# First block transpose behind the next step's sums, three thresholds taken from GpSimd, and the last batch's exponent step reordered, in a spectral-filter and soft-MoE kernel

## The chip, the core and the metric

The kernel runs on one core of a Trainium2 chip. The core has a matmul engine (TensorE, PE in the profile; its weight loads are listed apart as PEld), VectorE (DVE), ScalarE (ACT), GpSimd (POOL) and SyncE (SP), which here does nothing but issue transfers. The engines run their own instruction streams in order and wait for one another by semaphores. The metric is device time in microseconds (us) of one execution of the whole program; of several executions the median counts.

## The reference

Input `x` is 8 batches of 2496 tokens with 256 features.

```python
X = np.fft.rfft(x, axis=1)                       # along the tokens
Yr = Xr @ w_r - Xi @ w_i + b_r                   # 256 x 256 weights
Yi = Xr @ w_i + Xi @ w_r + b_i
Y  = sign(Y) * max(abs(Y) - 0.01, 0)             # on Yr and Yi apart
y  = np.fft.irfft(Y, n=2496, axis=1)             # 19968 x 256 when stacked
logits = y @ phi                                 # 32 slots, 4 for each of 8 experts
d = softmax over all 19968 tokens of logits
slot_input = d.T @ y
slot_out[e] = max(slot_input[e] @ w1[e], 0) @ w2[e]
c = softmax over the 32 slots of logits
out = c @ slot_out
```

## The kernel before

**Tiling.** The transform over 2496 tokens is split into one of 39 and one of 64 points. A batch b is 11 units of the first (`a_unit`, PE products `pa`, copied from PSUM to the SBUF tile `ast`, stored to DRAM as `adr`), then 5 steps of the second, each for 4 of the 20 frequencies k1 that are kept. Steps are numbered s = 5b + grp, with grp 0 to 4, 40 in all; in the tile names of an order listing `rt_1_0` is the tile of grp 1, half e = 0. Every batch but the first has its first-transform units run while the steps of the batch before run.

**A step.** `f2` makes the products `px` (two halves c of the features) from `ap`, which comes back from `adr`. ACT copies one part of `px` to `xsm` and rounds all of it to `xth`; DVE adds the other part to `xsm` ("the sums") and puts the rounding rest into `xtl`; POOL rounds `xsm` to `xsh` and puts the rest into `xsl`. Each product of 32-bit numbers is made of three products of rounded parts, so a rounded part and its rest always come in pairs (`xh`, `xl` of the input too: ACT writes `xh`, POOL `xl`). `lin_k` makes `pk` (12 matmuls from `xsh` and `xsl`), `lin_y` makes `py` for each half e of the 256 outputs (12 matmuls for e = 0, as many for e = 1) and DVE joins these and the bias into `ut`. Then comes the threshold sign(u) max(|u| - 0.01, 0), in one of two forms: on POOL, a `TENSOR_SCALAR` that clips `ut` to [-0.01, 0.01] and a `TENSOR_TENSOR` that subtracts this from `ut`; or a relu of `ut` - 0.01 on ACT (`ACTIVATE rt`) and then one `SCALAR_TENSOR_TENSOR` on DVE, min(`ut` + 0.01, relu), "the join". The table entry `lth` gives POOL and ACT in turn: in nearly all steps e = 0 goes the POOL way and e = 1 the ACT way. Only the last steps differ.

**After the threshold.** For the first three groups of the first seven batches the tile `rt` (threshold's result) has its 32 x 32 blocks transposed by a DVE `STREAM_TRANSPOSE` into `z`, one for each e; transfers `y<-z` (16 in a batch, issued by SP in `z_move`) complete the transposition. Of groups 3 and 4, PE transposes `rt` itself (`pt`, copied to `T`). `tp_p` makes the logits in the frequency domain (`pq`, scaled into `p_sb`). When a batch's five steps are through, `c_stages` carries them over to the tokens (`pg`, `pL`), finds the largest logit up to there (`pm`, then `mall` and the diagonal `dg`), spreads it over the partitions with a product with ones (`pb`), subtracts it (`ee`), takes the exponent (ACT `ACTIVATE ee`), goes back to frequencies (`pe`, `pd`, result `dd`) and sums the slots with the products `pr` of `dd` and `y` (or `T`). Of batch 7 `last_chain` does this without transfers between. The soft-MoE's experts and the output follow.

**What sets the order.** Each of these functions is a generator that yields a due time in units of its own (4 for a step, 20 for a batch) and then issues some instructions. A heap takes the earliest due time first. Every engine runs its instructions in the order in which they were issued (`_InOrder`, `sp`, `mm`), so a due time only moves instructions against one another in an engine's row; it delays nothing by itself. The due times are in the table `PLAN`. For this change: `zo`, added for the `z` transposes of e = 0 and e = 1 on top of `tlo`; `late['6']['pb']`, the due time of `pb` of batch 6; `T_['tl']`, the due times of the last step's joins. Helpers record the instructions, so nearly all rows of the profile name three lines: L227 (an instruction of DVE, ACT or POOL), L303 (a matmul) and L297 (a transfer of SP); L645 is a PE transpose.

Of the kernel before, what the change touches and what calls it, by code (L numbers as in the profile page):

```python
# [19 lines left out]
R, G = 3, 22  # L20
# [44 lines left out]
def _constants():  # L65
# [77 lines left out]
PLAN = {  # L143
    "ah": 'A',
    "al": 'P',
    "th": 'PA',
    "sh": 'P',
    "sl": 'P',
    "c0": 0.05,
    "pg": [1.35, 2.3],  # L150
    "pL": [6.6, 7.3],
# [14 lines left out]
    "ko": 0.915,  # L166
    "to": 0.4,
    "ws": [-29, -28.9, -28.8, 2],
    "late": {'6': {'cms': [13.1, 13.2, 18, 22.65, 22.66, 22.67], 'pd': [16.681, 16.6], 'pdt': ('pl', 'pl'), 'pr': [17.15, 18.3, 20.179, 19.707, 19.902], 'pL': [6.6, 7.3], 'pm': 8.51, 'pb': 9.45, 'pe': [11.747, 11.6, 12.419], 'pg': [0.875, 1.275], 'fr': {'sinv': 0, 'm2': 0, 'f1': 0, 'suni': 0}, 'pbx': 1.5, 'pet': ('pf', 'pf'), 'so': 0.2}, '5': {}, '4': {}},
    "T_": {'wl': [[-31, 't', 1], [-29.5, 't', 1], [-27.7, 't', 1], [-25.5, 't', 1], [-23.7, 't', 1], [-21.7, 't', 2], [-20.2, 't', 2], [-19.2, 't', 2], [-18.7, 't', 2], [-18.2, 't', 2], [-15.2, 't', 2], [-14.3, 't', 2], [-13.4, 't', 2], [-12.5, 'c', 2], [-11.8, 's', 1], [-11.2, 'a', 1], [-10.6, 'a', 1], [-10, 'a', 1], [-9.5, 'Ww_r', 1], [-8.7, 'Wnws', 1], [-8.6, 'Wwd', 1], [-6, 'Z', 1], [-5.9, 'Z', 1], [0.01, 'k', 1], [0.01, 'u', 1], [0.02, 'x', 2], [0.02, 'x', 2], [0.02, 'x', 2], [1.4, 'R', 2], [1.4, 'R', 2], [1.73, 'Z', 2], [1.74, 'Z', 2]], 'cl': 2.0, 'cp': 46.5, 'ct': 46.6, 'du': [[2.55, 2]], 'd1': [], 'cm': [19.9, 19.91, 19.92, 25, 25.1, 25.2], 'cm7': [0.71, 1.7, 1.95, 2.7, 2.71, 2.8], 'ye': 0.2, 'te': [[5.6, 0.2], [5.5, 0.4]], 'pg': [-15.49, -11.49, -7.99, -3.934, -2.9], 'yt': 0.578, 'wr': -30.6, 'tp': [0, 0.6, 0.85, 0.5], 'tt': [0.4, 0.55, 0.821, 1.25, 0.994], 'z': 1.686, 'th': [0.1, 0.12], 'tl': [0.2, 0.25], 'pgt': ['ps', 'ps', 'ps', 'pf', 'pf'], 'ch': [0.263, 0.5, 0.7, 1.0, 1.514, 2.0], 'te7': 'AAAAAAAAAA', 'op': 2, 'ot': [3, 5, 7], 'gt': [-14.5, -10.5, -7.0, -3.93, -2.89]},  # L170
    "f1": [-1.6, -1.5],
    "kw": [[-28.6, 4], [-28.4, 12]],
    "ap1": 1.85,
# [57 lines left out]
def fourier_soft_moe_kernel(ctx: ExitStack, tc: tile.TileContext, t: dict, out: bass.AP):  # L231
# [135 lines left out]
    ident, sgn, suni, sinv, dsc, dmask = (cols[k] for k in ("ident", "sgn", "suni", "sinv", "dsc", "dmask"))  # L367
    f1, m2 = cols["f1"][:P1], cols["m2"][:Q1]
# [146 lines left out]
    def moved(s):  # L515
        return s < NZ and s % NGRP < PLAN["nz"]
# [45 lines left out]
    def lin_y(s, e):  # L562
        b, grp = steps[s]
        end = s == ns - 1
        t0 = 4 * s + 1 + (PLAN["T_"]["ye"] if end else 1.35) * e
        yield t0
        py = psum("pl", f"py{b}_{grp}_{e}")
        lin(py, e, 0, xts[(s, 0)], 4 * 64 if grp else WH)
        if e == 1 and not end:
            t0 = 4 * s + 3  # L570
            yield t0
        lin(py, e, 1, xts[(s, 1)], 4 * 64 if grp else WH)
        t0 += 0.55 if e == 0 else PLAN["T_"]["yt"] if end else 0.3
        yield t0
        ks = kss[s]
        ut = wtile([128, KG, 2, 64], F32, "ut", f"ut{b}_{grp}_{e}")
        for ri in range(2):
            V.scalar_tensor_tensor(
                out=ut[:, :, ri, :],
                in0=py[:, ri * 256 : ri * 256 + 256].rearrange("p (j q) -> p j q", q=64),  # L580
                scalar=bcol[:, ri, e : e + 1],
                in1=ks[:, e, :].rearrange("p (j q) -> p j q", q=64),
                op0=ALU.add, op1=ALU.add,
            )
        if s >= NZ + 2:
# [541 lines left out]
    T_ = PLAN["T_"]  # L1127
# [223 lines left out]
    so = [wtile([128, D], F32R, "gp", f"so{i}") for i in range(2)]  # L1351
# [99 lines left out]
```

## Time and profile before

| | |
|---|---|
| median of 3 runs | 524.75 us (524.41, 524.75, 528.37) |
| the profiled execution | 523.68 us |
| its span (first to last instruction) | 521.9 us |
| what lies around the span | 1.8 us |
| busy: PE | 491.3 us, 94% of the span |
| busy: DVE, ACT, POOL | 352.5 us (68%), 327.0 us (63%), 316.6 us (61%) |
| transfers | 130.98 MB, 251 GB/s on the mean |

Busy time is the time in which an engine has an instruction at work. On PE matmuls overlap: a matmul with 256 columns is listed with 0.28 us and starts about 0.12 us behind the one before. A POOL `TENSOR_TENSOR` on 128x512 takes about twice as long as a DVE one of the same size (`xl` 1314 ns, `xtl` 680 ns on the mean).

### The profile page before, as it was taken

The numbers are of one execution on the slowest core, as the hardware profiler recorded it, in microseconds if no ns is written. First come the engines' busy times: TensorE is split into PE (matmuls) and PEld (weight loads), VectorE is DVE, ScalarE is ACT, GpSimd is POOL, SyncE is SP. The second block draws the span as 40 slices with busy tenths as digits, with TensorE's granted clock in tenths as the row PEclk, the third lists the DMA queues.
The fourth block names the chain that finished last, engine by engine and source line by source line (L and its number), as shares of the span: only waits on it lengthen the run. The fifth ranks groups of instructions, "written<-read, shape, count | busy, mean of one in ns | idle before, by whom it ended". The sixth has DMA issues, their size and how long they took to land.

```text
span 521.9 us, 11960 instructions
## 1 busy us (share of the span) xinstructions
PE 491.3 (94%) x4348; PEld 418.3 (80%) x4348; DVE 352.5 (68%) x703; ACT 327.0 (63%) x715; POOL 316.6 (61%) x367
## 2 busy tenths in 40 slices
PE   8887999999999999999999999999999979999991
PEld 4486899899789988998899898979888866468881
DVE  3255785688568866886688667966885686447671
ACT  4346467768666866687668766874565446247771
POOL 0048688778886797689868885887357413214210
PEclk9999899999999999999999999999999999999997
DMA  8998464579847895798589847974899989739998
GB/s 286 325 302 322 156 232 140 163 227 263 271 134 237 257 271 151 220 269 279 135 255 246 280 120 228 265 246 136 230 231 321 238 246 392 293 125 389 405 405 348
DMA packets 90318, 130.98 MB, mean 251 GB/s; under 512 B 40188, under 2 KB 61692, under 8 KB 90260
## 3 DMA queue, kind: packets, MB, share of 16 engines
q1 hardware_dynamic: 89316, 128.10, 76.9%
q10 hardware_dynamic: 944, 2.13, 1.2%
q8 instruction: 34, 0.56, 0.4%
q14 instruction: 24, 0.20, 0.1%
HBM read 69.19 MB, written 50.00 MB: 228 GB/s over the span
## 4 chain that ended last, share of the span: by engine, by line
PE 58%; DMA 15%; POOL 10%; ACT 5%; DVE 5%; issue 3%; SPq 3%; POOLq 0%; ACTq 0%; DVEq 0%
PE py L303 12%; PE pq L303 9%; PE px L303 8%; PE pa L303 8%; PE pk L303 5%; DMA w<-in_moe_w 3%; DMA gd<-g_sb 3%; PE pr L303 3%; POOL xl L227 3%; SPq L297 3%; POOL rt L227 2%; DMA gp<-gd 2%; PE pt L645 2%; POOL xsl L227 2%; PE pc L645 2%
## 5 line engine op out<-in xcount | busy, mean ns | idle before, releaser
L227 POOL TENSOR_TENSOR xl<-xr,xh 117x512 fp32r<-117x512 f32 x73 | 95.9, 1314 | 17.8 <-ACT xh L227 10.0
L303 PEld LDWEIGHTS px<-smov,ap 128*128 128x128 f32 x640 | 80.1, 192 | 10.9 <-ACT ast L227 6.2
L303 PE MATMUL px<-smov,ap 128*128 128x128 f32 x640 | 84.6, 276 | 3.6 <-ACT ast L227 3.6
L227 DVE SCALAR_TENSOR_TENSOR ut<-py,pk,k 128x256 f32<-128x256 f32 x160 | 69.7, 476 | 19.2 <-PE py L303 17.1
L227 POOL TENSOR_TENSOR xsl<-xsm,xsh 128x256 fp32r<-128x256 f32 x77 | 74.0, 961 | 6.3
L227 POOL CAST xsh<-xsm 128x256 fp32r<-128x256 f32 x78 | 34.8, 446 | 66.4 <-DVE xsm L227 53.5
L227 ACT COPY ast<-pa 128x512 f32<-128x512 f32 x82 | 48.4, 591 | 38.9 <-PE pa L303 37.7
L227 DVE STREAM_TRANSPOSE z<-rt 128x512 f32<-128x512 f32 x42 | 29.7, 706 | 38.6 <-POOL rt L227 24.1
L227 DVE TENSOR_TENSOR xtl<-px,xth 128x512 fp32r<-128x512 f32 x80 | 54.3, 680 | 0.1
L227 DVE TENSOR_TENSOR xsm<-px,xsm 128x256 f32<-128x256 f32 x80 | 33.3, 416 | 30.9 <-ACT xth L227 27.4
L303 PE MATMUL py<-xth,nwsh 128*128 128x256 f32 (+1 forms) x160 | 53.1, 332 | 0.4 <-ACT k L227 0.4
L227 ACT CAST xth<-px 128x512 fp32r<-128x512 f32 x80 | 47.3, 592 | 5.1 <-PE py L303 5.0
L227 POOL TENSOR_TENSOR rt<-ut,rt 128x512 f32<-128x512 f32 x39 | 50.1, 1286 | 0.2
L227 ACT COPY xsm<-px 128x256 f32<-128x256 f32 x80 | 30.0, 375 | 28.6 <-PE px L303 20.7
L303 PE MATMUL pk<-xsh,w_rh 128*128 128x256 f32 (+1 forms) x160 | 47.7, 298 | 0.2 <-POOL xsh L227 0.2
L227 ACT CAST xh<-xr 117x512 fp32r<-117x512 f32 x72 | 45.3, 631 | 2.9 <-DMA xr<-in_x 2.9
L303 PE MATMUL py<-xth,wdh 128*128 128x256 f32 (+1 forms) x160 | 45.2, 283 | 0.0
L303 PE MATMUL pk<-xsl,w_rh 128*128 128x256 f32 (+1 forms) x160 | 44.9, 281 | 0.3 <-POOL xsl L227 0.3
L303 PE MATMUL py<-xtl,wdh 128*128 128x256 f32 (+1 forms) x160 | 45.0, 281 | 0.0
L303 PE MATMUL py<-xtl,nwsh 128*128 128x256 f32 (+1 forms) x160 | 45.0, 281 | 0.0
L303 PE MATMUL py<-xth,wdl 128*128 128x256 f32 (+1 forms) x160 | 44.9, 281 | 0.0
L303 PE MATMUL py<-xth,nwsl 128*128 128x256 f32 (+1 forms) x160 | 44.8, 280 | 0.0
(223 smaller groups left out, 1307.0 us busy)
## 6 DMA issues: line engine op xcount, KB each, us to landing
ap<-adr SPq DMA_DIRECT2D x76, 256.0 KB
out<-ost SPq DMA_DIRECT2D x37, 512.0 KB
xr<-in_x SPq DMA_DIRECT2D x35, 512.0 KB
adr<-ast SPq DMA_DIRECT2D x20, 768.0 KB
y<-z SPq DMA_DIRECT2D x112, 96.0 KB
w<-in_moe_w SPq DMA_DIRECT2D x21, 512.0 KB
adr<-ast SPq DMA_DIRECT2D x7, 512.0 KB
w<-in_moe_w SPq DMA_DIRECT2D x14, 256.0 KB
```

Of the source, the lines that this page charges most:

```text
L227: return lambda *a, **k: self.tc.keep_in_program_order(f(*a, **k))
L297: sp_last.append(tc.keep_in_program_order(nc.sync.dma_start(**kw)))
L303: tc.keep_in_program_order(nc.tensor.matmul(**kw))
L645: tc.keep_in_program_order(nc.tensor.transpose(out=out, in_=in_, identity=identity))
```

## The change

Three entries of the table are edited, one is added, and two lines of `lin_y` use them:

- `zo` gets a third value: the first transpose of each batch (grp 0, e = 0) is due 1.5 units later, behind the sums of the step after the next.
- `hA`: 3 is new. In the steps 0, 1 and 2 (all of batch 0) the half e = 0 takes its threshold by ACT and DVE too, in place of POOL.
- `late['6']['pb']`: `pb` of batch 6 is due 0.91 units later.
- `T_['tl'][0]` goes from 0.2 to 0.24: the join of e = 0 in the very last step is due a little later. (The `T_` line is one long row of the table and is left out below.)

```diff
-    "late": {'6': {'cms': [13.1, 13.2, 18, 22.65, 22.66, 22.67], 'pd': [16.681, 16.6], 'pdt': ('pl', 'pl'), 'pr': [17.15, 18.3, 20.179, 19.707, 19.902], 'pL': [6.6, 7.3], 'pm': 8.51, 'pb': 9.45, 'pe': [11.747, 11.6, 12.419], 'pg': [0.875, 1.275], 'fr': {'sinv': 0, 'm2': 0, 'f1': 0, 'suni': 0}, 'pbx': 1.5, 'pet': ('pf', 'pf'), 'so': 0.2}, '5': {}, '4': {}},
+    "late": {'6': {'cms': [13.1, 13.2, 18, 22.65, 22.66, 22.67], 'pd': [16.681, 16.6], 'pdt': ('pl', 'pl'), 'pr': [17.15, 18.3, 20.179, 19.707, 19.902], 'pL': [6.6, 7.3], 'pm': 8.51, 'pb': 10.36, 'pe': [11.747, 11.6, 12.419], 'pg': [0.875, 1.275], 'fr': {'sinv': 0, 'm2': 0, 'f1': 0, 'suni': 0}, 'pbx': 1.5, 'pet': ('pf', 'pf'), 'so': 0.2}, '5': {}, '4': {}},
...
-    "zo": [0.7, 1.0],
+    "zo": [2.2, 0.7, 1.0],
     "nz": 3,
+    "hA": 3,
...
         yield t0 + (PLAN["T_"]["th"][e] if end else PLAN["tho"])
-        relu = L_("th", s, e) is A
+        relu = s < PLAN["hA"] or L_("th", s, e) is A
         if relu:
             A.activation(out=rt, in_=ut, func=AF.Relu, bias=nlam)
...
         if moved(s):
-            yield t0 + PLAN["tlo"] + PLAN["zo"][e]
+            yield t0 + PLAN["tlo"] + PLAN["zo"][0 if grp == e == 0 else e + 1]
```

One line more in the table moves the helpers' lines by one: L227 becomes L228, L303 becomes L304.

DVE in batch 0, from the second `ut` of step 0 on, before:

```order
L227 SCALAR_TENSOR_TENSOR ut_0_1_393<-py_0_1_364,pk_110,k_0_323 128x4x64 x2
L227 STREAM_TRANSPOSE z_404<-rt_0_0_352 128x4x128
L227 TENSOR_TENSOR xsm_2_0_430<-px_2_0_406,xsm_2_0_430 128x256
L227 TENSOR_TENSOR xtl_2_0_429<-px_2_0_406,xth_2_0_428 128x512
L227 SCALAR_TENSOR_TENSOR rt_0_1_396<-ut_0_1_393,rt_0_1_396 128x512
L227 SCALAR_TENSOR_TENSOR ut_1_0_463<-py_1_0_438,pk_110,k_1_436 128x4x64 x2
L227 STREAM_TRANSPOSE z_404<-rt_0_1_396 128x4x128
L227 TENSOR_TENSOR xsm_2_1_502<-px_2_1_468,xsm_2_1_502 128x256
L227 TENSOR_TENSOR xtl_2_1_501<-px_2_1_468,xth_2_1_500 128x512
L227 SCALAR_TENSOR_TENSOR ut_1_1_534<-py_1_1_478,pk_110,k_1_436 128x4x64 x2
L227 TENSOR_TENSOR p_sb_490<-pq_0_491,pk_110 128x128
L227 STREAM_TRANSPOSE z_404<-rt_1_0_466 128x4x128
```

And the same stretch of DVE after:

```order
L228 SCALAR_TENSOR_TENSOR ut_0_1_392<-py_0_1_364,pk_110,k_0_323 128x4x64 x2
L228 SCALAR_TENSOR_TENSOR rt_0_0_352<-ut_0_0_349,rt_0_0_352 128x512
L228 TENSOR_TENSOR xsm_2_0_428<-px_2_0_404,xsm_2_0_428 128x256
L228 TENSOR_TENSOR xtl_2_0_427<-px_2_0_404,xth_2_0_426 128x512
L228 SCALAR_TENSOR_TENSOR rt_0_1_395<-ut_0_1_392,rt_0_1_395 128x512
L228 STREAM_TRANSPOSE z_461<-rt_0_0_352 128x4x128
L228 SCALAR_TENSOR_TENSOR ut_1_0_463<-py_1_0_436,pk_110,k_1_434 128x4x64 x2
L228 STREAM_TRANSPOSE z_461<-rt_0_1_395 128x4x128
L228 TENSOR_TENSOR xsm_2_1_502<-px_2_1_468,xsm_2_1_502 128x256
L228 TENSOR_TENSOR xtl_2_1_501<-px_2_1_468,xth_2_1_500 128x512
L228 SCALAR_TENSOR_TENSOR ut_1_1_533<-py_1_1_478,pk_110,k_1_434 128x4x64 x2
L228 SCALAR_TENSOR_TENSOR rt_1_0_466<-ut_1_0_463,rt_1_0_466 128x512
```

The first transpose (of `rt_0_0`) has moved behind the sums of step 2 and the join `rt_0_1`, and joins `rt_0_0` and `rt_1_0` are new on DVE. `rt_2_0` gets one as well. On POOL the two instructions of each of these three thresholds are gone, and ACT has three `ACTIVATE rt` more.

DVE in batch 2, where its first transpose stands, before:

```order
L227 TENSOR_TENSOR p_sb_1180<-pq_4_1805,pk_110 128x128
L227 STREAM_TRANSPOSE z_1883<-rt_0_0_1784 128x4x128
L227 TENSOR_TENSOR xsm_2_0_1913<-px_2_0_1885,xsm_2_0_1913 128x256
L227 TENSOR_TENSOR xtl_2_0_1912<-px_2_0_1885,xth_2_0_1911 128x512
L227 SCALAR_TENSOR_TENSOR rt_0_1_1861<-ut_0_1_1858,rt_0_1_1861 128x512
L227 SCALAR_TENSOR_TENSOR ut_1_0_1951<-py_1_0_1923,pk_110,k_1_1921 128x4x64 x2
L227 STREAM_TRANSPOSE z_1883<-rt_0_1_1861 128x4x128
```

And after:

```order
L228 TENSOR_TENSOR p_sb_1180<-pq_4_1805,pk_110 128x128
L228 TENSOR_TENSOR xsm_2_0_1911<-px_2_0_1883,xsm_2_0_1911 128x256
L228 TENSOR_TENSOR xtl_2_0_1910<-px_2_0_1883,xth_2_0_1909 128x512
L228 SCALAR_TENSOR_TENSOR rt_0_1_1861<-ut_0_1_1858,rt_0_1_1861 128x512
L228 STREAM_TRANSPOSE z_1949<-rt_0_0_1784 128x4x128
L228 SCALAR_TENSOR_TENSOR ut_1_0_1951<-py_1_0_1921,pk_110,k_1_1919 128x4x64 x2
L228 STREAM_TRANSPOSE z_1949<-rt_0_1_1861 128x4x128
```

Here nothing is added: the transpose changes places with the sums (`xsm`, `xtl`) and the join `rt_0_1`. The batches 1 to 6 all read like this one; POOL's order there is the same as before.

PE at the end of the steps, where `pb` of batch 6 stands, before (from the end of the products `py` of grp 3 on):

```order
L303 MATMUL py_3_1_6291<-xth_3_1_6171,wdl 128x256
L303 MATMUL py_3_1_6291<-xtl_3_1_6172,wdh 128x256
L303 MATMUL pb_6354<-dg_6332,ones 117x32
L645 MATMUL pq_2_6303<-pk_110,lg_2_6345 128x128
L303 MATMUL pk_4_6365<-xsh_4_0_6231,w_rh 128x256
L303 MATMUL pk_4_6365<-xsh_4_0_6231,w_rl 128x256
```

And after, from the last `pk` on:

```order
L304 MATMUL pk_4_6360<-xsh_4_1_6322,w_rh 128x256
L304 MATMUL pk_4_6360<-xsh_4_1_6322,w_rl 128x256
L304 MATMUL pk_4_6360<-xsl_4_1_6323,w_rh 128x256
L304 MATMUL pb_6373<-dg_6332,ones 117x32
L304 MATMUL py_4_0_6385<-xth_4_0_6228,nwsh 128x256
L304 MATMUL py_4_0_6385<-xth_4_0_6228,nwsl 128x256
```

`pb` has moved from ahead of the transposition in `pq` and the 12 `pk` to behind these.

ACT in the same stretch (thresholds of the last steps, exponents `ee` and `fo` of batch 6, the copies `eT` behind the products `pe`), before:

```order
L227 ACTIVATE rt_2_0_6133<-ut_3_1_6349,nlam 128x512
L227 COPY k_4_6383<-pk_4_6365 128x512
L227 ACTIVATE ee_6358<-ee_6358 117x704
L227 ACTIVATE fo<-fo 128x1
L227 ACTIVATE rt_2_0_6133<-ut_4_0_6422,nlam 128x512
L227 COPY eT_6426<-pe_0_6427 128x20x12 x2
L227 COPY eT_6426<-pe_1_6428 128x2x20x3
```

And after:

```order
L228 ACTIVATE rt_2_0_6133<-ut_3_1_6349,nlam 128x512
L228 COPY k_4_6383<-pk_4_6360 128x512
L228 ACTIVATE rt_2_0_6133<-ut_4_0_6420,nlam 128x512
L228 ACTIVATE ee_6375<-ee_6375 117x704
L228 ACTIVATE fo<-fo 128x1
L228 COPY eT_6430<-pe_0_6431 128x20x12 x2
L228 COPY eT_6430<-pe_1_6432 128x2x20x3
```

The relu of the last step's first half now stands ahead of the exponents. On DVE, `p_sb` has moved ahead of `ee` and `fo`, and the last `ut` ahead of the join of the half before it. SP's order is unchanged.

## Rows read from the trace of the kernel before

**Rows 1.** Stretches: us, PE, PEld, DVE, ACT, POOL busy (count), PEclk, DMA share, GB/s

```profile
52.50:57.00 4.50, 4.50 (x19) 4.07 (x20) 2.33 (x5) 1.10 (x2) 2.99 (x4) 0.62 0.44 179
115.00:167.00 52.00, 50.95 (x471) 45.60 (x470) 37.79 (x76) 36.87 (x80) 40.80 (x45) 1.00 0.76 226
374.00:433.00 59.00, 54.29 (x598) 46.87 (x597) 42.40 (x88) 31.62 (x79) 29.36 (x39) 1.00 0.91 262
```

**Rows 2.** Waits of PE between 40 and 63 us: total, times, longest

```profile
PE pa L303 <- DVE ast L227: 1.8, 1, 1.8
PE pa L303 <- ACT k L227: 1.5, 1, 1.5
```

**Rows 3.** Waits of PE between 130 and 370 us

```profile
PE px L303 <- ACT ast L227: 3.4, 5, 0.7
PE pa L303 <- POOL xl L227: 0.8, 3, 0.3
```

**Rows 4.** Chain that ended last, batch 0: start, us, what

```profile
46.90 0.58 POOL rt L227
47.48 1.26 POOL xl L227
...
49.16 0.72 POOL xsl L227
49.88 1.24 POOL rt L227
...
51.78 0.66 DVE ast L227
...
52.48 0.97 PE pa L303 x3
```

**Rows 5.** Timeline, batch 2: start, us, engine, operation, [idle before, releaser]

```profile
137.04 0.59 ACT L227 CAST xth<-px 128x512 fp32r<-128x512 f32 x1
...
138.51 0.72 POOL L227 TENSOR_TENSOR dd<-dd,pk 128x320 f32<-128x320 f32 x1
...
139.19 1.29 POOL L227 TENSOR_TENSOR xl<-xr,xh 117x512 fp32r<-117x512 f32 x1
...
140.31 0.71 DVE L227 STREAM_TRANSPOSE z<-rt 128x512 f32<-128x512 f32 x1 [3.88 <-DMA y<-z]
...
141.86 0.67 DVE L227 SCALAR_TENSOR_TENSOR rt<-ut,rt 128x512 f32<-128x512 f32 x1
141.88 1.24 POOL L227 TENSOR_TENSOR xsl<-xsm,xsh 128x256 fp32r<-128x256 f32 x1
```

**Rows 6.** Tile `xsl` on POOL: ns shortest/median/longest, first and last start

```profile
L227 POOL TENSOR_TENSOR xsl<-xsm,xsh x77: 727/746/1257, 36.1 to 414.1; 128x256 fp32r<-128x256 f32 x77
```

**Rows 7.** Timeline, batch 6, the same place

```profile
347.13 0.91 DVE L227 SCALAR_TENSOR_TENSOR rt<-ut,rt 128x512 f32<-128x512 f32 x1
347.45 1.17 POOL L227 TENSOR_TENSOR dd<-dd,pk 128x320 f32<-128x320 f32 x1
```

**Rows 8.** Timeline, last steps and behind them

```profile
420.91 0.39 PE L303 MATMUL pb<-dg,ones 128*117 128x32 f32 x2 [1.04 <-DVE dg L227]
...
421.16 0.87 DVE L227 SCALAR_TENSOR_TENSOR ut<-py,pk,k 128x256 f32<-128x256 f32 x2
...
422.70 0.28 PE L303 MATMUL py<-xth,nwsh 128*128 128x256 f32 x1
...
423.44 0.80 ACT L227 ACTIVATE ee<-ee 117x704 f32<-117x704 f32 x1
...
424.42 0.88 DVE L227 SCALAR_TENSOR_TENSOR ut<-py,pk,k 128x256 f32<-128x256 f32 x2 [0.73 <-ACT fo L227]
...
425.33 0.72 ACT L227 ACTIVATE rt<-ut,nlam 128x512 f32<-128x512 f32 x1 [1.00 <-DVE ut L227]
...
425.63 0.62 PE L303 MATMUL pe<-pk,ee 117*32 117x120 f32 x16
...
433.02 1.29 PE L303 MATMUL pr<-y,dd 128*32 128x256 f32 x20 [0.20 <-DMA w<-in_moe_w]
```

More of the change, by code (lines that the diff above doesn't have):

```diff
@@ L168 @@
     "ws": [-29, -28.9, -28.8, 2],
-    "late": {'6': {'cms': [13.1, 13.2, 18, 22.65, 22.66, 22.67], 'pd': [16.681, 16.6], 'pdt': ('pl', 'pl'), 'pr': [17.15, 18.3, 20.179, 19.707, 19.902], 'pL': [6.6, 7.3], 'pm': 8.51, 'pb': 9.45, 'pe': [11.747, 11.6, 12.419], 'pg': [0.875, 1.275], 'fr': {'sinv': 0, 'm2': 0, 'f1': 0, 'suni': 0}, 'pbx': 1.5, 'pet': ('pf', 'pf'), 'so': 0.2}, '5': {}, '4': {}},
-    "T_": {'wl': [[-31, 't', 1], [-29.5, 't', 1], [-27.7, 't', 1], [-25.5, 't', 1], [-23.7, 't', 1], [-21.7, 't', 2], [-20.2, 't', 2], [-19.2, 't', 2], [-18.7, 't', 2], [-18.2, 't', 2], [-15.2, 't', 2], [-14.3, 't', 2], [-13.4, 't', 2], [-12.5, 'c', 2], [-11.8, 's', 1], [-11.2, 'a', 1], [-10.6, 'a', 1], [-10, 'a', 1], [-9.5, 'Ww_r', 1], [-8.7, 'Wnws', 1], [-8.6, 'Wwd', 1], [-6, 'Z', 1], [-5.9, 'Z', 1], [0.01, 'k', 1], [0.01, 'u', 1], [0.02, 'x', 2], [0.02, 'x', 2], [0.02, 'x', 2], [1.4, 'R', 2], [1.4, 'R', 2], [1.73, 'Z', 2], [1.74, 'Z', 2]], 'cl': 2.0, 'cp': 46.5, 'ct': 46.6, 'du': [[2.55, 2]], 'd1': [], 'cm': [19.9, 19.91, 19.92, 25, 25.1, 25.2], 'cm7': [0.71, 1.7, 1.95, 2.7, 2.71, 2.8], 'ye': 0.2, 'te': [[5.6, 0.2], [5.5, 0.4]], 'pg': [-15.49, -11.49, -7.99, -3.934, -2.9], 'yt': 0.578, 'wr': -30.6, 'tp': [0, 0.6, 0.85, 0.5], 'tt': [0.4, 0.55, 0.821, 1.25, 0.994], 'z': 1.686, 'th': [0.1, 0.12], 'tl': [0.2, 0.25], 'pgt': ['ps', 'ps', 'ps', 'pf', 'pf'], 'ch': [0.263, 0.5, 0.7, 1.0, 1.514, 2.0], 'te7': 'AAAAAAAAAA', 'op': 2, 'ot': [3, 5, 7], 'gt': [-14.5, -10.5, -7.0, -3.93, -2.89]},
@@ new lines @@
+    "late": {'6': {'cms': [13.1, 13.2, 18, 22.65, 22.66, 22.67], 'pd': [16.681, 16.6], 'pdt': ('pl', 'pl'), 'pr': [17.15, 18.3, 20.179, 19.707, 19.902], 'pL': [6.6, 7.3], 'pm': 8.51, 'pb': 10.36, 'pe': [11.747, 11.6, 12.419], 'pg': [0.875, 1.275], 'fr': {'sinv': 0, 'm2': 0, 'f1': 0, 'suni': 0}, 'pbx': 1.5, 'pet': ('pf', 'pf'), 'so': 0.2}, '5': {}, '4': {}},
+    "T_": {'wl': [[-31, 't', 1], [-29.5, 't', 1], [-27.7, 't', 1], [-25.5, 't', 1], [-23.7, 't', 1], [-21.7, 't', 2], [-20.2, 't', 2], [-19.2, 't', 2], [-18.7, 't', 2], [-18.2, 't', 2], [-15.2, 't', 2], [-14.3, 't', 2], [-13.4, 't', 2], [-12.5, 'c', 2], [-11.8, 's', 1], [-11.2, 'a', 1], [-10.6, 'a', 1], [-10, 'a', 1], [-9.5, 'Ww_r', 1], [-8.7, 'Wnws', 1], [-8.6, 'Wwd', 1], [-6, 'Z', 1], [-5.9, 'Z', 1], [0.01, 'k', 1], [0.01, 'u', 1], [0.02, 'x', 2], [0.02, 'x', 2], [0.02, 'x', 2], [1.4, 'R', 2], [1.4, 'R', 2], [1.73, 'Z', 2], [1.74, 'Z', 2]], 'cl': 2.0, 'cp': 46.5, 'ct': 46.6, 'du': [[2.55, 2]], 'd1': [], 'cm': [19.9, 19.91, 19.92, 25, 25.1, 25.2], 'cm7': [0.71, 1.7, 1.95, 2.7, 2.71, 2.8], 'ye': 0.2, 'te': [[5.6, 0.2], [5.5, 0.4]], 'pg': [-15.49, -11.49, -7.99, -3.934, -2.9], 'yt': 0.578, 'wr': -30.6, 'tp': [0, 0.6, 0.85, 0.5], 'tt': [0.4, 0.55, 0.821, 1.25, 0.994], 'z': 1.686, 'th': [0.1, 0.12], 'tl': [0.24, 0.25], 'pgt': ['ps', 'ps', 'ps', 'pf', 'pf'], 'ch': [0.263, 0.5, 0.7, 1.0, 1.514, 2.0], 'te7': 'AAAAAAAAAA', 'op': 2, 'ot': [3, 5, 7], 'gt': [-14.5, -10.5, -7.0, -3.93, -2.89]},
```

## Prediction

> **What bounds the kernel now.** I read first the busy shares by stretch. PE is busy 50.95 of 52 us in a stretch of one batch (115 to 167 us) [rows 1], at a granted clock of 1.00, which is its 2.4 GHz level; DVE, ACT and POOL stand at 71 to 78% of it. So a change of DVE's or POOL's order counts only where PE waits, or comes to wait. The second view is PE's waits. In 130 to 370 us, nearly five batches, they are small: 3.4 us for `px` behind `ast`, 0.8 us for `pa` behind POOL's `xl` [rows 3]. The first is the turnaround of a copy and lies on ACT, which the change doesn't touch there. The second tells that POOL's row reaches PE at one place in some batches, with nothing to spare. In batch 0, 40 to 63 us, PE waits 1.8 us in one piece for `pa` behind DVE's copy `ast`, and 1.5 us for `k` on ACT [rows 2]. The third view, the chain that ended last, says what the 1.8 us are: POOL `xl` from 47.48, `xsl` from 49.16, the subtraction `rt` from 49.88 for 1.24; to 51.12; then DVE `z`, whose `ast` follows at 51.78, and PE `pa` at 52.48 [rows 4]. DVE stood idle in front of `z`, with `ast` queued behind it. Right behind, from 52.50 to 57.00, the granted clock is 0.62 on the mean, PE at its lower level (1.2 GHz) for much of it [rows 1].
>
> **Thresholds of batch 0 (`hA`).** Three thresholds leave POOL (six instructions) and become an `ACTIVATE` (0.72 us, [rows 8]) and a join on DVE (0.67, [rows 5]) each. What counts is `rt_1_0`, the tile that this `z` waited for. By the new order DVE has this join right behind `ut` and `p_sb` of the step. POOL's clip, 0.58 us at 46.90 [rows 4], no longer stands ahead of `xl`, so `xl` that ended at 48.74 (47.48 + 1.26) ends at about 48.15. The join reads two tiles in SBUF, as do POOL's `TENSOR_TENSOR`s, and rows 5 and 7 show that these don't run side by side; so I let it run behind `xl`, 48.15 to 48.8, then `z` (0.71) to 49.5 and `ast` (0.66) to 50.15. POOL's `xsl` stays about where it was, ending at 49.88, as the 0.6 us gained go to the join. PE is at `pa` only when the products `pk` behind `xsl` are through, at about 50.7 (52.48 less the wait of 1.8). `ast` is there some 0.5 us before. So **-1.8 us** of wait.
>
> With it the clock: 4.5 us at 0.62 lose (1 - 0.62) x 4.5 = 1.7 us [rows 1]. The dip stands just behind this wait, and ahead of it is also the 1.5 us for `k`, which stays. I take it that without the 1.8 us the dip goes: **-1.7 us**; the other bound is 0 (it comes anyway, behind the wait for `k`). The three `ACTIVATE`s lie on an engine that waits for PE's `pk` there (`k` follows `pk`) and cost nothing; if one came in front of `k`, 0.72. Batch 0: **-3.5 us**, between -1.1 and -3.5.
>
> **First transposes behind the sums (`zo`).** In batches 2 to 5 the transpose `z` waits for its tile (`y<-z` transfers of the batch before must have left it), 3.88 us of idle DVE in batch 2, ending at 140.31 [rows 5]; behind it stand the sums, `xsm`, `xtl`, and the join. These are what the move sets free. But who waits for them? POOL takes `xsh` only behind a second `dd` that follows `xl` (139.19 + 1.29), so the sums some 3 us sooner are of no use to it, and `px`, `pk` and `py` of the next step are far from late. So I cost the gain on PE at nothing; the cover is POOL's own row, which is busy without a gap from `dd` to `xl` to `dd` here. If that cover were gone, `pa <- xl` is what could improve, 0.8 us in all [rows 3].
>
> What comes with it: the sums now start when ACT's `xth` is there, at 137.63 (137.04 + 0.59), take 1.0 together (`xtl` 0.68 on the mean, `xsm` has half its elements) and so the join falls to about 138.65. Before, it ran at 141.86, against `xsl`, which took 1.24 us instead of the usual 0.75 [rows 5, 6]. Now it meets POOL's `dd` (138.51 for 0.72) and stands ahead of `xl` (139.19), for which PE waits [rows 3, 5]. The same meeting can be seen in batch 6 as it is: the join at 347.13 has 0.91 us, as it starts while `xl` still runs, and `dd` at 347.45 then 1.17 instead of 0.72 [rows 7]. So the join, if it comes while `dd` runs, waits for its end and then holds up `xl` by what it lasts. From the rows the price of one such meeting is 1.24 - 0.746 = 0.50 us [rows 5, 6], and PE has no slack ahead of `xl`. By where the rows stand I count this in batches 2, 3, 4 and 6; in batch 5 `xl` has already started, and in batch 1 the transpose waits for POOL's `rt` and hardly at all. **+2.0 us** (4 x 0.50). The bounds: 0 (the join slips into a gap, or `xl` is first and `pa` starts on time), and five whole joins, 5 x 0.67 = 3.4 us.
>
> The Trainium skill ("SBUF — State Buffer", section "Who interferes with whom") says that a DVE instruction with two SBUF inputs contends with a GpSimd instruction that reads SBUF, and that whoever comes first has the shared ports for the whole instruction while the other is fully blocked. The rows agree that one waits, but `xsl` lost 0.50 us and not the 0.67 of the join. By the rule to the letter the four meetings would cost 4 x 0.67 = 2.7 us, by the row 2.0; it speaks against this part of the change either way.
>
> **The tail (`pb`, `tl`).** `pb` made PE wait 1.04 us at 420.91 [rows 8]. Behind the 12 `pk` its `dg` is long there. But the gain is not that 1.04: `py` of the last step, which came at 422.70, needs the PSUM bank that `ut` leaves at 422.03 (421.16 + 0.87), so it comes at about 422.07: -0.63. Then on ACT: the relu of the last step's first half now stands ahead of the exponents. Its 12 `py` from 422.07 on, 0.12 apart, end at 423.7, so `ut` (0.88) at about 424.6; the relu takes 0.72 to 425.3, `ee` 0.80 to 426.1, and `pe`, which started at 425.63, waits for `ee` and comes at 426.1: **+0.48 us**. This shift runs on to `pr` at 433.02. That one waited 0.20 us for a transfer of weights [rows 8], so 0.2 are absorbed: **+0.3 us**, bounds -0.6 (the relu ends as early as `py` gains) and +0.5.
>
> **Sum.** -3.5 + 2.0 + 0.3 = -1.2 us against the profiled 523.68, of which 521.9 are span: 522.5. The median of the runs is 1.07 us above the profiled execution, so the forecast is **523.5 us**. A measurement of this kernel tells 1%, 5.2 us, from no change (below 519.5 or above 530.0): by this, no change.
>
> **Rivals.** All on the median, 524.75.
>
> - *The meetings don't bite.* The join finds POOL between two instructions, or `xl` is first. For it: in batch 5 that is what I expect, and a join that came 0.6 us later would do no harm to `xl`; against: POOL has no gaps there [rows 5]. -3.5 + 0.3: 521.5 us. Chance 22%.
> - *The move also clears PE.* With the sums early, POOL's row comes loose and the waits for `xl` vanish too (-0.8, [rows 3]); the tail gains its whole wait, -1.04. -3.5 - 0.8 - 1.04 = -5.3: 519.4 us. Against: POOL waits for nothing but itself in rows 5. Chance 8%.
> - *Transfers take it all.* From 374 to 433 the transfers stand at 0.91 of the 16 engines, and `pr` waited for a landing [rows 1, 8]. If the weights land no sooner, what PE gains or loses before is made up there, and only the tail's rest shows: 525.0 us. Against: 0.20 us is a short wait, and the loads' start hangs on buffers that come free earlier too. Chance 12%.
> - *Slower: the join in front of `xl`.* The mechanism of the +2.0, at its full price in all five batches from 2 to 6 (3.35), with the tail at +0.5 and the clock still falling in batch 0 (-1.8 there): +2.05, 526.8 us. It decides from the point where the meetings cost more than batch 0 gives, seven at 0.50, or the five with the clock not won back. Chance 10%.
> - *`hA` doesn't do its work.* The wait of `pa` stays, since the join `rt_1_0` is held by POOL up to behind `xsl` (49.88) and `z` and `ast` end only at 51.9, or ACT's relu is late. Then the 1.8 shrinks to 0.5, the clock falls: -0.5 + 2.0 + 0.3: 526.5 us. Chance 5%.
>
> **Numbers.** The forecast has 43%: with its own bounds some 522 to 525. The range of 519.8 to 526.9 holds all cases but the second rival and the outer end of the slower ones. Faster by over 1%: half of the second rival, and what of the first ends as low, 0.07. Slower by over 1% needs meetings at more than twice their price: 0.03. Within 1%: 0.90.
>
> **What would show it.** In the profile after: no wait of `pa` behind `ast` around 50.5 us, and PEclk near 1.00 in 52 to 57; if the wait is gone and the clock still falls, the 1.7 were wrong. In batches 2 to 6: DVE's idle time ahead of the first `z` gone, the join next to `dd` with one of them stretched, and PE's waits for `xl` grown from 0.8 to nearly 3 us; if they stay at 0.8, the meetings don't bite. In the tail: no wait at `pb`, a wait of about 1 us at `pe` for `ee`, `pr` behind 433.0 by as much as the rest doesn't shift it. The prediction is wrong as a whole if PE's waits in 130 to 370 us fall instead of rising, or if the time behind 433 us, which the change doesn't touch, differs.

## The result: 1.2% faster, and the profile after

The changed kernel takes 519.38 us at the median of 6 runs (517.36 to 520.09); the kernel before took 524.58 us at the median of 6 (523.77 to 528.37). The ratio of the mean times is 0.9882, 95% interval 0.9847 to 0.9917. Here and below, a ratio leaves out executions that took over 1.5% longer than the fastest of their kernel, and a median does not. The profiled execution took 519.74 us, its span is 517.9 us, against 523.68 and 521.9 before. The forecast of 523.5 us was too high, and the time lies below its range.

PE's order is the same in both kernels but for the one `pb`, so each matmul of the trace after has its partner in the trace of before. The difference of their starts, read along the program, tells where time came from or went. At these places (named by their time before) it is, in us:

| before, us | 49.94 `pk` | 56.93 `px` | 115.9 `px` | 348.9 `px` | 415 | 433.0 `pr` | last matmul |
|---|---|---|---|---|---|---|---|
| changed kernel | -2.32 | -5.92 | -5.60 | -7.69 | -4.53 | -3.91 | -3.86 |

**Batch 0.** PE's waits between 40 and 63 us, and the stretch behind the place of the old wait (columns as in rows 1), in the kernel after:

```profile
PE pk L304 <- POOL xsl L228: 0.3, 1, 0.3
```

```profile
48.30:52.80 4.50, 4.50 (x37) 4.11 (x39) 3.32 (x7) 2.17 (x5) 3.36 (x4) 1.00 0.81 320
```

Both waits of [rows 2] are gone, and PEclk is 1.00 where it was 0.62 [rows 1]. The chain that ended last, in the kernel after, goes through PE itself now, where it went through POOL and DVE [rows 4]:

```profile
46.84 0.74 POOL xsl L228
...
47.62 0.74 PE pk L304 x4
48.35 0.70 PE pa L304 x3
49.05 1.42 PE py L304 x12
```

From 49.94 to 56.93 this is -3.60 us. The -2.32 ahead of it are another thing: ACT's `xh` waited for a transfer there, 2.91 us in the execution before and 1.62 us in this one, and the wait for `k` hangs on it. In the traces of the twelve other kernels below this place lies between -1.04 and +1.42 us, with and without each of the edits, so the -2.32 can't be put down to the change.

**The steady stretch.** PE's waits in the kernel after from 125 to 365 us (the work of 130 to 370 before):

```profile
PE pa L304 <- POOL xl L228: 2.1, 3, 0.8
PE pL L304 <- ACT chpL L228: 1.1, 2, 1.0
PE pd L304 <- POOL clpd L228: 0.3, 1, 0.3
```

The waits for `xl` rose from 0.8 to 2.1 us, as forecast. But the five of `px` behind `ast`, 3.4 us [rows 3], are gone. The timeline of batch 2 after shows both (compare rows 5):

```profile
133.01 0.68 DVE L228 TENSOR_TENSOR xtl<-px,xth 128x512 fp32r<-128x512 f32 x1
133.46 0.72 POOL L228 TENSOR_TENSOR dd<-dd,pk 128x320 f32<-128x320 f32 x1
...
133.61 1.12 DVE L228 SCALAR_TENSOR_TENSOR rt<-ut,rt 128x512 f32<-128x512 f32 x1
...
134.14 1.72 POOL L228 TENSOR_TENSOR xl<-xr,xh 117x512 fp32r<-117x512 f32 x1
...
135.92 0.50 PE L304 MATMUL pa<-xl,f1h 117*128 117x512 f32 x1 [0.77 <-POOL xl L228]
...
136.48 1.06 PE L304 MATMUL px<-smov,ap 128*128 128x128 f32 x8
...
136.68 0.58 ACT L228 COPY ast<-pa 128x512 f32<-128x512 f32 x1 [1.55 <-PE pa L304]
```

The meeting is there as foretold: the join comes at `dd`, lasts 1.12 us, and `xl` 1.72 instead of 1.29. But then `px` starts at 136.48, before the copy `ast` has even begun (136.68). So `px` can't have needed that copy in this kernel. In the kernel before, the same matmuls stood like this:

```profile
140.53 0.50 PE L303 MATMUL pa<-xl,f1h 117*128 117x512 f32 x1 [0.33 <-POOL xl L227]
...
141.26 0.67 DVE L227 TENSOR_TENSOR xtl<-px,xth 128x512 fp32r<-128x512 f32 x1
141.31 0.59 ACT L227 COPY ast<-pa 128x512 f32<-128x512 f32 x1 [1.14 <-PE pa L303]
...
141.95 1.16 PE L303 MATMUL px<-smov,ap 128*128 128x128 f32 x8 [0.68 <-ACT ast L227]
```

From `pa` to `px` it was 1.42 us and is 0.56 now: 0.86 us less, and 0.82 to 0.94 less in each of the other four batches (3 to 6). Note that `xtl` (141.93) and `ast` (141.90) both ended just ahead of `px`.

**The tail.** In the kernel after, timeline:

```profile
414.31 0.32 PE L768 MATMUL pm<-pk,mx 117*128 117x117 f32 x1 [0.51 <-ACT gT L228]
...
417.66 0.36 PE L304 MATMUL py<-xth,nwsh 128*128 128x256 f32 x1 [0.64 <-DVE ut L228]
...
420.36 0.72 ACT L228 ACTIVATE rt<-ut,nlam 128x512 f32<-128x512 f32 x1 [1.62 <-DVE ut L228]
420.99 0.77 ACT L228 ACTIVATE ee<-ee 117x704 f32<-117x704 f32 x1
...
421.82 1.34 PE L304 MATMUL pe<-pk,ee 117*32 117x120 f32 x48 [1.08 <-ACT ee L228]
```

No wait at `pb`; instead `py` waits for `ut` and `pe` for `ee`, behind the relu [rows 8]. Between 348.9 and 415 the changed kernel gives back 3.2 us in this execution: `pd` of batch 5 waits three times, 1.7 us together (one of 0.7 us stood there before too), the first as its input `eb` comes late from DRAM, and then PEclk is 0.50 for 3.40 us, which is 1.7 us lost:

```profile
383.57 0.46 ACT L228 CAST chpd<-eb 128x320 fp32r<-128x320 f32 x1 [3.06 <-DMA eb<-ed]
```

```profile
386.70:390.10 3.40, 3.40 (x18) 3.39 (x17) 1.14 (x3) 1.59 (x4) 3.32 (x4) 0.50 1.06 260
```

### The profile page after: what moved, and what is told of

Read it like the earlier page. It is cut to its first block, busy times and chain, and to the rows that moved or that the text cites. A ratio compares the mean times of both kernels' runs of the same rounds, so it can differ in the third digit from the quotient of the medians.

```text
span 517.9 us, 11977 instructions
## 1 busy us (share of the span) xinstructions
PE 490.0 (95%) x4348; PEld 418.9 (81%) x4348; DVE 360.1 (70%) x706; ACT 328.4 (63%) x718; POOL 311.5 (60%) x361
## 4 chain that ended last, share of the span: by engine, by line
PE 61%; DMA 15%; POOL 8%; DVE 5%; ACT 4%; issue 2%; SPq 2%; ACTq 0%; POOLq 0%; DVEq 0%
PE py L304 13%; PE pq L304 9%; PE px L304 9%; PE pa L304 8%; PE pk L304 6%; PE pr L304 3%; DMA eb<-ed 3%; POOL xl L228 2%; DMA w<-in_moe_w 2%; SPq L298 2%; DMA ed<-ea 2%; PE pt L646 2%; PE pc L646 2%; DMA gd<-g_sb 2%; POOL rt L228 2%
## 5 line engine op out<-in xcount | busy, mean ns | idle before, releaser
L228 POOL TENSOR_TENSOR xl<-xr,xh 117x512 fp32r<-117x512 f32 x73 | 96.8, 1327 | 15.3 <-ACT xh L228 8.1
L304 PEld LDWEIGHTS px<-smov,ap 128*128 128x128 f32 x640 | 81.2, 193 | 5.8 <-ACT ast L228 0.7
L304 PE MATMUL px<-smov,ap 128*128 128x128 f32 x640 | 85.0, 277 | 0.3 <-ACT ast L228 0.3
L228 DVE SCALAR_TENSOR_TENSOR ut<-py,pk,k 128x256 f32<-128x256 f32 x160 | 69.5, 475 | 20.1 <-PE py L304 17.6
L228 POOL CAST xsh<-xsm 128x256 fp32r<-128x256 f32 x78 | 36.0, 462 | 67.7 <-DVE xsm L228 53.0
L228 POOL TENSOR_TENSOR xsl<-xsm,xsh 128x256 fp32r<-128x256 f32 x77 | 72.1, 936 | 6.3
L228 ACT COPY ast<-pa 128x512 f32<-128x512 f32 x82 | 48.3, 590 | 36.1 <-PE pa L304 34.9
L228 DVE TENSOR_TENSOR xsm<-px,xsm 128x256 f32<-128x256 f32 x80 | 33.4, 417 | 42.2 <-ACT xth L228 35.8
L228 DVE TENSOR_TENSOR xtl<-px,xth 128x512 fp32r<-128x512 f32 x80 | 54.2, 679 | 0.1
L304 PE MATMUL py<-xth,nwsh 128*128 128x256 f32 (+1 forms) x160 | 53.0, 331 | 1.0 <-DVE ut L228 0.6
L228 ACT CAST xth<-px 128x512 fp32r<-128x512 f32 x80 | 47.3, 592 | 5.1 <-PE py L304 5.1
L304 PE MATMUL pk<-xsh,w_rh 128*128 128x256 f32 (+1 forms) x160 | 48.1, 300 | 0.0
L228 ACT CAST xh<-xr 117x512 fp32r<-117x512 f32 x72 | 45.4, 632 | 1.6 <-DMA xr<-in_x 1.6
L228 POOL TENSOR_TENSOR rt<-ut,rt 128x512 f32<-128x512 f32 x36 | 46.3, 1287 | 0.1
L304 PE MATMUL pk<-xsl,w_rh 128*128 128x256 f32 (+1 forms) x160 | 45.3, 283 | 0.4 <-POOL xsl L228 0.3
L304 PE MATMUL py<-xth,wdh 128*128 128x256 f32 (+1 forms) x160 | 44.9, 281 | 0.0
L304 PE MATMUL pk<-xsh,w_rl 128*128 128x256 f32 (+1 forms) x160 | 44.9, 281 | 0.0
L304 PE MATMUL py<-xtl,nwsh 128*128 128x256 f32 (+1 forms) x160 | 44.8, 280 | 0.0
L304 PE MATMUL py<-xtl,wdh 128*128 128x256 f32 (+1 forms) x160 | 44.7, 280 | 0.0
L304 PE MATMUL py<-xth,nwsl 128*128 128x256 f32 (+1 forms) x160 | 44.7, 279 | 0.0
L304 PE MATMUL py<-xth,wdl 128*128 128x256 f32 (+1 forms) x160 | 44.6, 279 | 0.0
L228 ACT COPY xsm<-px 128x256 f32<-128x256 f32 x80 | 30.0, 375 | 23.0 <-PE px L304 15.3
```

What stands on the lines that cost most here:

```text
L228: return lambda *a, **k: self.tc.keep_in_program_order(f(*a, **k))
L304: tc.keep_in_program_order(nc.tensor.matmul(**kw))
```

## Why px no longer waits: another PSUM bank

The order of the instructions doesn't show it, but the built programs do (the lists `SECOND` below are made from them): in batches 2 to 6 the second half's `px` of grp 2 lies in another PSUM bank. PSUM is the memory that PE writes its products to. Tiles of the tag `pf` share two banks, and the pool picks one for each tile when it is issued. Before, that `px` got the bank of `pa` and waited for its copy `ast`. After, it gets the bank of the first half's `px`, and has to wait for what reads this, the sums last. With the transpose moved, the pool picks differently, and from there on the two banks are swapped for many later tiles; a swap of both by itself only renames them. My theory then: **the steady gain is this bank together with the early sums**; the meetings at `xl` take part of it. Rivals: batch 0 gives all of the gain; or the early sums help without the bank, or the bank without them.

## Experiments

Ratios are to the kernel before, timed on the same chip in turn.

**Each edit alone.** `z_alone` has the `zo` edit only:

```diff
-    "zo": [0.7, 1.0],
+    "zo": [2.2, 0.7, 1.0],
-            yield t0 + PLAN["tlo"] + PLAN["zo"][e]
+            yield t0 + PLAN["tlo"] + PLAN["zo"][0 if grp == e == 0 else e + 1]
```

> Only the first transpose of each batch is moved (zo); thresholds and tail as before. Theory (early sums give PE's px its PSUM bank sooner): the five waits of px behind the copy ast (3.4 us in 130 to 370 us, 0.85 us each from start to start in the trace of after) go, three to four waits for POOL xl grow by 0.45 us each, so about -2.5 us: 522.1 us. Rival (the steady stretch gains nothing by this edit, all of the gain comes from batch 0): between 0 and +2 us, as the prediction had it: 524.6 to 526.6 us, with the waits of px still there.

Measured: 0.9956 (0.9925 to 0.9988), -2.3 us. PE's waits, 125 to 365 us, have no `px` behind `ast`, and more of `xl`:

```profile
PE pa L303 <- POOL xl L227: 2.3, 3, 0.8
PE px L303 <- DMA ap<-adr: 1.1, 1, 1.1
```

From 115.9 to 348.9 its trace gains 2.19 us, as the changed kernel's does (2.09). The edit that I had put at +2.0 us is a gain.

`h_alone` has the `hA` edit only:

```diff
+    "hA": 3,
-        relu = L_("th", s, e) is A
+        relu = s < PLAN["hA"] or L_("th", s, e) is A
```

> Only the three thresholds of batch 0 are moved to ScalarE and VectorE (hA). Theory: PE's wait of 1.8 us for pa behind ast in batch 0 goes and the dip of the granted clock behind it with it: -3.5 us, 521.1 us; the five waits of px in 130 to 370 us stay at 3.4 us. If the 1.5 us for k is shortened by this edit too (it is gone in the trace of after), -4.5 to -5 us: 519.9 us. Rival (batch 0 gives little, the gain is in the steady stretch): -1 us or less.

Measured: 0.9954 (0.9922 to 0.9986), -2.4 us. From 49.94 to 56.93 its trace gains 3.60 us, the very number of the changed kernel (all nine traces with `hA` gain 3.3 to 3.6 there); the waits of `px` in the steady stretch are untouched:

```profile
PE px L304 <- ACT ast L228: 3.4, 5, 0.7
PE pa L304 <- POOL xl L228: 0.5, 2, 0.3
```

`tail_alone`:

```diff
-'pb': 9.45
+'pb': 10.36
-'tl': [0.2, 0.25]
+'tl': [0.24, 0.25]
```

> Only pb of batch 6 behind pk and the last ut ahead of the join (pb and tl). The trace of after has PE gain 1.1 us at the place of pb, lose 0.9 us of it again at py of the last step (behind ut) and lose 1.2 us more at pe behind ee. Theory: +1.0 us, 525.6 us. Rival, the prediction's term: +0.3 us, 524.9 us. Rival 2 (a transfer behind it sets the time): 0.

Measured: 0.9993 (0.9958 to 1.0028): no difference to be seen; the interval holds +1.0, +0.3 and 0, and the medians, 525.05 us against 523.31, don't speak for 0. Its trace loses 0.7 us from 415 to `pe`, and 0.8 more at `pr`, which waits 1.1 us for a transfer of weights where it was 0.2.

`z_and_h` has the diffs of `z_alone` and `h_alone`, with the old tail.

> The transposes and the thresholds moved, the tail as before. Theory (the tail costs 1.0 us): -6.2 us against before, 518.4 us, a little faster than the changed kernel. Rival (the tail as changed gains or is free): 519.4 us or more.

Measured: 0.9881 (0.9837 to 0.9925), -6.2 us, the ratio of the changed kernel. So the two edits carry the whole gain, and the tail's part is too small for a timing.

**The bank.** `old_banks` is the changed kernel, `new_banks` the kernel before, each with the tiles of `pf` and `pt` pinned to the banks of the other. All five engines' orders stay as they were. `SECOND` lists the names of the tiles in the second bank. It moves other tiles of the two tags as well; that `px` is the one that counts is read from PE's waits:

```diff
     def psum(tag, name):
+        if tag in ("pf", "pt") and name in SECOND:
+            tag += "2"
...
-    psum_bufs = {"pf": 2, "pl": 2, "pt": 2, "ps": 1, "pr": 1}
+    psum_bufs = {"pf": 1, "pf2": 1, "pl": 2, "pt": 1, "pt2": 1, "ps": 1, "pr": 1}
```

> The changed kernel with every engine's order as it is, but each tile of the PSUM tags pf and pt is pinned to the bank that it has in the kernel before: px of the third group's second half is again written over the bank of pa, behind the copy ast, in place of the bank of px of the first half. Theory (the gain of the steady stretch is this bank together with the early sums): the five waits of px behind ast come back, 0.85 us each from start to start, so +4.2 us on the changed kernel: about -1.5 us against before, and the waits for xl stay at about 2 us. Rival (the early sums help by themselves, the bank is a side effect): the px waits stay away, -5.2 us against before.

Measured: 0.9991 (0.9960 to 1.0022): with the old bank the whole change is worth nothing that can be timed. The expected -1.5 us lies inside the interval; the interval of the changed kernel (up to 0.9917) does not meet it. PE's waits in `old_banks`, 125 to 365 us:

```profile
PE px L309 <- ACT ast L231: 3.4, 5, 0.7
PE pa L309 <- POOL xl L231: 1.6, 2, 0.8
PE px L309 <- DMA ap<-adr: 1.1, 1, 1.1
```

The five waits are back, to the tenth of a microsecond. From 115.9 to 348.9 this trace loses 2.39 us, where the changed kernel gains 2.09: 4.5 us between the two, of which the five `px` are 4.25. In two traces whose steady stretch is that of the kernel before (`h_alone`, `tail_alone`) it came out 0.6 and 0.8 us shorter, so differences of less than 1 us mean little here. The early sums alone do nothing for PE. The 2.39 are its waits: 0.8 more for `xl`, 1.1 for `ap`, a transfer that is late in six of the traces, and 0.5 in two smaller ones.

> The kernel before with its orders as they are, but the tiles of pf and pt pinned to the banks that they have in the changed kernel, so that px waits for the sums of the first half and not for the copy ast. Theory (bank and early sums are needed together): the sums end at 141.93 us there, the copy at 141.90, so the five waits of px stay, now behind xtl: 0 us (within 0.5). Rival (the bank alone does it): -4 us.

Measured: 0.9975 (0.9949 to 1.0001), -1.3 us, just about no difference. PE's waits in `new_banks`, 125 to 365 us, and `px` in batch 2 with the sums ahead of it:

```profile
PE px L308 <- ACT chpg L230: 1.0, 1, 1.0
PE pL L308 <- ACT chpL L230: 0.8, 2, 0.5
PE pa L308 <- POOL xl L230: 0.6, 2, 0.3
PE px L308 <- ACT ast L230: 0.6, 1, 0.6
PE px L308 <- DVE xtl L230: 0.4, 1, 0.4
```

```profile
138.19 0.71 DVE L230 STREAM_TRANSPOSE z<-rt 128x512 f32<-128x512 f32 x1 [4.05 <-POOL xl L230]
...
139.13 0.67 DVE L230 TENSOR_TENSOR xtl<-px,xth 128x512 fp32r<-128x512 f32 x1
...
139.95 1.13 PE L308 MATMUL px<-smov,ap 128*128 128x128 f32 x8 [0.98 <-ACT chpg L230]
```

`px` waits here too, up to the end of `xtl`, which stands behind the late `z`. The view names `chpg`, as that ended in the same moment (139.95), while `xtl` ended at 139.80. The three waits of `px` that the table puts down to `chpg`, `ast` and `xtl` (batches 2, 4 and 5) are one kind: each time `px` starts 0.15 us behind the end of `xtl`, and the `chpg` and the `ast` named ended only as it started. So three of the five waits stayed, now behind the sums, 2.0 us in place of 3.4; in batches 3 and 6 there is none. The bank alone helps some: its trace gains 1.64 us from 115.9 to 348.9, about 1 us more than `h_alone` and `tail_alone` with nothing changed there. The expected 0 (within 0.5) was too strict; the rival's -4 us is out.

**The meetings at xl.** `z_between` is `z_alone` with the first transpose between the sums and the join, so that the join comes later:

```diff
-    "zo": [2.2, 0.7, 1.0],
+    "zo": [1.87, 0.7, 1.0],
```

> As z_alone, but the first transpose is put between the sums and the join (zo 1.87 in place of 2.2), so that the join comes 0.7 us later, when POOL's xl has started. Theory (the join at POOL's dd delays xl, 0.45 us in three batches): the waits of pa for xl fall from 2.3 back to 0.8 us or less, the px waits stay away: 1.4 us less than z_alone, about -3.5 us against before. Rival (the join held behind xl now holds POOL's next steps or delays ut instead): the same as z_alone, or worse.

Measured: 0.9899 (0.9864 to 0.9934). PE's waits, 125 to 365 us:

```profile
PE pa L303 <- POOL xl L227: 0.8, 3, 0.3
PE px L303 <- DMA ap<-adr: 0.6, 1, 0.6
```

The waits for `xl` are back at the 0.8 of before, and those of `px` stay away. In batch 2 POOL's `xl` has 1.29 us again, starting ahead of the join:

```profile
139.93 1.29 POOL L227 TENSOR_TENSOR xl<-xr,xh 117x512 fp32r<-117x512 f32 x1
...
141.05 0.71 DVE L227 STREAM_TRANSPOSE z<-rt 128x512 f32<-128x512 f32 x1 [1.56 <-DMA y<-z]
...
141.68 0.77 DVE L227 SCALAR_TENSOR_TENSOR rt<-ut,rt 128x512 f32<-128x512 f32 x1
```

From 115.9 to 348.9 this trace gains 5.25 us, 3.1 more than `z_alone`; 1.5 of these are the `xl` waits and 0.5 a shorter wait for `ap`. The rest is not the place of the transpose: the five other traces with it between sums and join (`zh_between` and the four of the tail below) gain 2.7 to 4.2 us, 3.8 on the mean of all six, against 2.2 on the mean of the three with it behind the join (the changed kernel, `z_alone`, `z_and_h`). That is 1.5 us, what the `xl` waits give.

`zh_between` adds the diff of `h_alone` to it, with the old tail.

> The transposes between sums and join and the thresholds of batch 0 moved, the tail as before. Theory: what z_between and h_alone give together, -3.5 - 2.3 = -5.8 us at least, and as z_and_h gave -6 with the join in front of xl, some -7 us against before; faster than the changed kernel. Rival: like z_and_h, -6 us.

Measured: 0.9853 (0.9815 to 0.9892), 516.72 us; run again on another chip as `tail_before`, 0.9902 (0.9868 to 0.9936), 518.67 us. The same kernel in two timings is 2 us apart, so the -7.7 us of the first is not to be taken by itself.

**The tail.** Three variants on top of `zh_between`, timed together with it (`tail_before`). `tail_pb` has the first two lines of the diff of `tail_alone`, `tail_pb_tl` all four.

> zh_between once more (transposes between sums and join, thresholds of batch 0 moved, tail as in the kernel before), as the base for the three others on the same chip: -7 us against before.

> As tail_before, with pb of batch 6 due 0.91 later, which also takes the last step's first relu ahead of the exponents on ScalarE; the joins as before. Theory (pb gains 0.2 on PE, since py then waits for ut; the relu ahead of ee costs 1.2 at pe): +1.0 us on tail_before. Rival, the prediction's term: +0.3. Rival 2 (pr behind it waits for transfers anyway): 0.

> As tail_pb, and the last ut ahead of the join (tl), so the changed kernel's whole tail. Theory (the join waits for ScalarE's relu, ut no longer stands behind it, but pe has waited by then): the same as tail_pb, within 0.3 us; +1.0 us on tail_before.

> As tail_pb, but the exponents keep their due time (pbx 0.59 in place of 1.5), so that they stand ahead of the last step's relu on ScalarE as before. Theory (the relu is what costs): pe waits no more for ee, -0.2 us on tail_before, 1.2 us less than tail_pb. Rival (ee itself is late, as its pb is later by the 12 pk): +0.5 us on tail_before.

`tail_pb_exp` is `tail_pb` with one more number:

```diff
-'pbx': 1.5
+'pbx': 0.59
```

Ratios: 0.9902, 0.9906 (0.9871 to 0.9942), 0.9889 (0.9853 to 0.9924) and 0.9877 (0.9840 to 0.9915). The timings don't tell them apart, the traces do. By the difference of starts, from 415 to 433 us, `tail_before` loses 0.1 us against before, `tail_pb` and `tail_pb_tl` 0.6 each, and `tail_pb_exp` gains 0.4: 0.5 worse than `tail_before`, and 0.5 better. Expected were +1.0 (or the prediction's +0.3) for the first two and -0.2 for the third: the signs are the theory's, the sizes lie between the two for `tail_pb`. PE's waits from 408 to 425 us in `tail_pb`:

```profile
PE pe L304 <- ACT ee L228: 1.1, 1, 1.1
...
PE py L304 <- DVE ut L228: 0.7, 1, 0.7
```

and in `tail_pb_exp`:

```profile
PE pq L646 <- ACT lg L228: 0.9, 1, 0.9
PE py L304 <- DVE ut L228: 0.7, 1, 0.7
```

The wait of `pe` goes when the exponents keep their place ahead of the relu. So the relu's place was its cause, it came with `pb` (the exponents are due 1.5 behind it), and `tl` is worth nothing on PE (`tail_pb_tl` loses the same 0.6 as `tail_pb`).

## Why the prediction was wrong

- **The step that failed** is in the part on `zo`: "So I cost the gain on PE at nothing", resting on the sentence that the wait of `px` behind `ast` "is the turnaround of a copy and lies on ACT, which the change doesn't touch there". The change did touch it, as it gave that `px` another bank. The bank of `pa`'s copy was a choice of the pool and not a need of the kernel. `old_banks` shows what the change does without that: no gain at `px`, and no difference in the time that can be seen. That it lost 2.39 us in the steady stretch where I had said +2.0 is luck in part, as only 0.8 of them are waits for `xl`. In place of +2.0 the term measured -2.1 us: -4.25 from `px` (5 x 0.85), +1.3 from the waits for `xl`, the rest smaller waits that differ between executions. PE's waits in 130 to 370 us fell from 4.2 to 3.5 us, which the prediction had named as the sign that it is wrong as a whole.
- **The meetings at `xl`** were right in kind, and near in place and price: `xl` is 0.43 us longer in batches 2, 3 and 6. There were three of them and not four, +1.3 us on PE's waits in place of +2.0; in batch 4 `xl` kept its length and the join took 1.52 us. The price is not a fixed 0.50. In batch 2 the join ended at 134.73 and `xl` 1.13 us later, 0.16 less than its 1.29 alone; in rows 5 `xsl` ended 0.59 us behind the join, 0.16 less than its usual 0.75. So in both meetings the POOL instruction lost the time from its start to the join's end, less 0.16 us.
- **Batch 0** was right for the profiled execution, -3.60 us from 49.94 to 56.93 where I had said -3.5, but the clock's part of it was too sure. All five traces without `hA` have the wait for `ast` (1.3 us in `z_alone`, 1.7 to 1.8 in the others), and three of them the low clock behind it. `new_banks` has PEclk 1.00 there, and so has `z_alone`, whose low stretch stood earlier; but `z_between` and `tail_alone` had one earlier and this one as well. With `hA` no trace has one there. From 49.94 to 56.93 the four other traces without `hA` differ from that of before by -2.2, -1.5, -0.4 and -0.2 us, -0.85 on the mean of five, so the edit gives -3.6 + 0.85 = -2.75 us on the mean; `h_alone` timed -2.4. The term that was too large is the clock's, by these five traces some 1.0 us (3/5 x 1.7, an estimate) in place of 1.7.
- **The tail** measured +0.7 at `pe` (the same in all five traces that have `pb` late and `ee` behind the relu), where I had said +0.48, and +0.6 at `pr`, just outside its bounds of -0.6 to +0.5. The mechanism was right: `py` and `pe` wait as foretold. But `ut` cost 0.9 us at `py`, so that of the gain of 1.4 us ahead of it 0.5 was left, and the relu then took 1.2 at `pe`. One thing may speak for the new tail: behind the 1.0 us that `pb` waits with the old one, two of eight traces (`z_alone`, `z_and_h`) have 3.4 us at half clock and lose 1.5 us by it, and none of the six with `pb` late has. So few traces don't show that it is the pause.
- **Rivals.** "The move also clears PE" named 519.4 us, the time measured, by luck: it had the waits for `xl` vanish, which grew, and the tail gain its whole wait, where it lost. "Transfers take it all" did not come as stated, as `pr` waited 0.2 us as before. But a late transfer ahead of it cost the profiled execution part of the 3.2 us that it lost at `pd` and behind it; of the twelve others only `z_and_h` shows the like (2.7 us, in an execution of 523.83 us where its median is 517.69), the rest at most 0.6.
- **What stays open:** how the runs of the changed kernel share out the -5.2 us of the medians. The traces give -2.75 (batch 0 on the mean), -2.1 and +0.6, together -4.25; the rest (1 us, or 2 by the ratio of the means) is not accounted for, and traces of the same order differ by as much: 2.7 to 5.25 us in the steady stretch alone.

## What to carry to other kernels

A wait for a buffer is only as fixed as the allocation: before costing a moved step, compare not only the order of the instructions but also which buffer each tile gets and what each instruction waits for, since a due time that moves one release can hand later tiles another bank. When two candidates ended within some 0.15 us of the end of a wait, look at both: in `new_banks` the view named the wrong one. And a step that is moved can be put to use twice: here the transposition between the sums and the join (`z_between`, 0.9899) looks like a better place than the one the change gave it (`z_alone`, 0.9956), though the intervals just touch; with `hA` that gave 0.9853 and 0.9902 in two timings, and 0.9877 with `pb` late and the exponents kept in place; the intervals overlap that of the changed kernel, so none is shown to beat it.

## What of the hardware was not expected

The low clock moves about between executions of nearly the same work. A stretch of 3.4 us at 1.2 GHz stood at about 18, 35, 44, 53, 388 or 420 us, depending on the execution, twice or more in four traces (`z_alone`, `tail_alone`, `z_between`, `z_and_h`), and in three (`new_banks`, `tail_before`, `tail_pb_tl`) nowhere ahead of the last 11 us. The one at 53 stood behind the pause of 1.7 to 1.8 us, in three of the five traces that wait there; the one at 387 in the changed kernel behind three waits of 0.6, 0.4 and 0.7 us; those at 420 behind a wait of 1.0 us, which six other traces have without a fall. One trace's low stretch belongs in a sum with a chance beside it.
